# Attention and gated feed-forward on one core: batches 0 and 1 by head halves and tile pairs, w_out loaded in one go, a new order table

## The chip, the cores and the metric

The kernel runs on one core of one Trainium2 chip. The metric is the device time of one execution in microseconds; the median of 3 runs of the kernel before is 281.9 us (281.62 to 282.12).

## What is computed

For each of 8 batches and 8 heads, a linear attention with position weights: q and k go through a ReLU and are multiplied by cos and sin of the position, so that 64 features become 128; kv is the sum over the sequence of k' times v, z the sum of k'; each output row is q' kv / (q' z + 1e-6). The heads side by side are a token's 512 values x, for 8 x 576 = 4608 tokens. Then a feed-forward layer with a gate:

```python
q_p = phi(q, cos_w, sin_w)
k_p = phi(k, cos_w, sin_w)
kv = np.einsum('bhsf,bhsd->bhfd', k_p, v)
z = np.sum(k_p, axis=2)
num = np.einsum('bhsf,bhfd->bhsd', q_p, kv)
den = np.einsum('bhsf,bhf->bhs', q_p, z)[..., None] + 1e-06
x = (num / den)          # to (4608, 512)
h = x @ w_in             # (512, 2048)
out = (h * np.cos(h)) @ w_out   # (2048, 512)
```

## The kernel before

The feed-forward layer runs over nine chunks of 512 tokens: four tiles of 128 from each of the eight batches, and a ninth chunk of what is left of all of them. `layer1(c)` multiplies chunk c by w_in and applies the gate (ACT computes cos as a shifted Sin, L502; DVE or GpSimd multiplies, L504); `layer2(c)` multiplies by w_out. From chunk 3 on parts of layer 1, and from chunk 1 on all of layer 2, save products in Strassen's manner with sums made ahead (`w_out_sums`, L809; L861 and L667 are those matmuls). Layer 1 of chunks 0 and 1 (L529) works in 16 groups of eight matmuls of 256 columns: per quarter of w_in, per half of the tokens, two column pairs. The three banks M1 of PSUM are used in turn. Layer 2 of chunk 0 is plain (`layer2_plain`, L786): eight groups of eight matmuls of 512 columns, four token tiles for the first half of w_out and four for the second; ACT copies the first (L794), DVE adds the second (L797).

A batch's attention: SyncE (SP) loads q, k and v (`load`, two DMAs each, L318 and L321; v of batches 0 and 1 in head halves, four DMAs). `prep` (L346 on ACT, L347 on DVE) makes q' and k' in f16, one instruction per tile and factor with all 8 heads (128x512); `cast_v` (L360 to L362) makes v in f16. PE transposes q' (L402), forms kv (L373) and the numerators with z in a 65th column (L435); DVE normalises (L451 adds 1e-6, L453 inverts, L455 multiplies); PE transposes x (L475) and ACT copies it to xT (L479). From batch 2 on the DMA transposes q' and, later, x.

The beginning: `first_attention` (batch 0) loads q, k and v and has PE run fill matmuls on a constant tile (`warm`, L945) where it would be idle. `weights` holds w_in's four quarters, loaded by GpSimd (POOL) with a cast (L956), until batch 0's keys have landed: a small copy (L950) writes into w_in_sb and reads the keys, so that the DMA waits for it. In the same way a copy (L960) lets w_out's first two quarters go (L970) when w_in's first quarter has landed. `second_attention` (batch 1) holds its loads by small copies on POOL that read w_in's third quarter (`hold_raw`, L975; `GATE1`), and w_out's last two quarters by one that reads batch 1's queries (`part_of_w_out`, L982).

The order of all work is written out by hand. Every step is recorded by `pl.add` with an engine or a choice of them, what it reads and what it writes; `Plan.run` sorts the 1363 steps by the table STARTS and takes each one's engine from the table ENGS. Each engine then runs its steps in that order, one after the other, and waits by semaphores for what a step reads. PE, ACT, DVE, POOL and SP have one queue each; the DMAs that SP issues run in the profile's queue 1, those of POOL in queue 0.

## Time and profile before

| what | value |
|---|---|
| median of 3 runs | 281.9 us (281.62 to 282.12) |
| the profiled execution, from its first to its last instruction (its span; its own time is listed as no more than this) | 279.7 us |
| median above that span | 2.2 us |
| PE busy | 272.6 us (97%) |
| DVE / ACT / POOL busy | 236.9 / 210.2 / 82.9 us |
| granted TensorE clock | 1.000 |
| batch 0's first layer-1 matmul | 21.20 us |
| PE without interruption on layer 1 of batch 0 from | 23.88 us |
| batch 1's first layer-1 matmul | 50.27 us |
| chain: last PE work to the end of the span | 273.27 to 279.7 us |
| w_in issued by POOL | 11.13 to 14.58 us |
| w_out issued by POOL | 17.75 to 19.23 us and 38.49 to 40.15 us |
| batch 1's loads issued by SP | 25.88 to 33.81 us |

The page gives busy time per engine, the chain of work that ended last (followed back from the last instruction, at each step to what released it), groups of instructions by source line, and the DMA issues with their time to landing. Answers about a part of the trace give the same for a stretch: the timeline merges instructions of one line on one engine, and gives in brackets the idle time of the engine before them and what ended it; "SPq" and "POOLq" are DMA issues. In `x8` at a line's end, 8 is a count.

### The profile page before, as it was taken

What the parts mean: (1) busy time and instruction counts of PE and PEld (TensorE: products, weight loads), DVE (VectorE), ACT (ScalarE), POOL (GpSimd) and SP (SyncE); (2) the same over time, 40 slices, a digit from 0 to 9 for tenths busy, and PEclk for the clock granted to TensorE, in tenths of its full rate; (3) what the DMA queues carried; (4) which work ended last, traced back from release to release, by engine and by line L of the source; (5) the groups of instructions that cost most, each with busy time, mean ns of one, the idle gap of its engine ahead of it and who ended that gap; (6) DMA issues with size and microseconds to landing.
All of it is one profiled execution on the core that took longest, in us unless ns stands there. A gap on an engine that the chain in (4) does not pass through costs nothing.

```text
span 279.7 us, 6825 instructions
## 1 busy us (share of the span) xinstructions
PE 272.6 (97%) x2698; PEld 215.5 (77%) x2698; DVE 236.9 (85%) x442; ACT 210.2 (75%) x363; POOL 82.9 (30%) x102
## 2 busy tenths in 40 slices
PE   8999999999999999999999999999999999999993
PEld 2567857787966677769777878789988888888882
DVE  1767698989999999999999998989989879873952
ACT  2756699879998897788989988995758686776330
POOL 1430020030501201520340045132534372399210
PEclk9999999999999999999999999999999999999999
DMA  6999989999999999989999998549756495698125
GB/s 207 312 202 206 340 239 241 361 301 174 335 261 271 258 249 246 234 268 259 255 258 246 242 229 284 98 115 141 163 75 139 110 156 105 152 143 123 75 77 150
DMA packets 80223, 58.03 MB, mean 207 GB/s; under 512 B 43200, under 2 KB 77248, under 8 KB 80192
## 3 DMA queue, kind: packets, MB, share of 16 engines
q1 hardware_dynamic: 68960, 39.99, 59.4%
q0 software_dynamic: 10496, 17.04, 30.1%
q10 hardware_dynamic: 736, 0.57, 0.7%
q8 instruction: 21, 0.34, 0.5%
q14 instruction: 10, 0.08, 0.1%
HBM read 36.75 MB, written 11.80 MB: 174 GB/s over the span
## 4 chain that ended last, share of the span: by engine, by line
PE 92%; ACT 3%; DVE 2%; issue 1%; POOL 0%; ACTq 0%; POOLq 0%
PE M L861 34%; PE M L667 14%; PE M L561 11%; PE M L529 9%; PE TR L667 6%; PE ATT L945 5%; PE ATT L435 3%; PE M L786 3%; PE ATT L373 3%; PE TR L561 2%; ACT KQ L346 2%; DVE x L455 1%; PE M L402 1%; PE M L373 0%; PE TR L475 0%
## 5 line engine op out<-in xcount | busy, mean ns | idle before, releaser
L861 PEld LDWEIGHTS <-gT 128*128 128x128 f16 x560 | 53.9, 98 | 8.3
L861 PE MATMUL M<-w_out_sb,gT 128*128 128x256 f16 x448 | 57.1, 273 | 0.0
L504 DVE TENSOR_TENSOR gT<-M,ch 128x512 f16<-128x512 f32 x73 | 48.5, 685 | 5.9 <-ACT ch L502 5.7
L502 ACT ACTIVATE ch<-M 128x512 f32<-128x512 f32 x75 | 43.4, 596 | 12.0 <-PE M L529 5.4
L346 ACT ACTIVATE KQ<-km,CS 128x512 f16<-128x512 f32 x57 | 38.5, 717 | 1.4 <-DMA km<-in_k_dram 1.3
L872 ACT ACTIVATE ost<-M 128x512 f32<-128x512 f32 x41 | 24.3, 596 | 17.9 <-PE M L861 13.0
L346 ACT ACTIVATE KQ<-qm,CS 128x512 f16<-128x512 f32 x46 | 31.5, 720 | 4.1 <-DMA qm<-in_q_dram 4.1
L561 PE MATMUL M<-xT,w_in_sb 128*128 128x512 f16 x136 | 33.8, 379 | 0.0
L861 PE MATMUL M<-T,S 128*128 128x256 f16 x256 | 32.4, 273 | 0.0
L667 PEld LDWEIGHTS <-w_in_sb 128*128 128x128 f16 x288 | 27.3, 98 | 4.8 <-issue 0.3
L362 POOL CAST V<-vm 128x1024 f16<-128x1024 f32 (+1 forms) x18 | 15.9, 907 | 50.8 <-DVE den L451 20.7
L529 PE MATMUL M<-xT,w_in_sb 128*128 128x256 f16 x256 | 30.3, 273 | 0.3 <-DVE gT L504 0.3
L861 PEld LDWEIGHTS <-S 128*128 128x128 f16 x256 | 24.8, 98 | 4.1 <-DVE S L837 0.2
L529 PEld LDWEIGHTS <-w_in_sb 128*128 128x128 f16 x256 | 24.4, 98 | 3.9 <-issue 0.5
L679 DVE TENSOR_TENSOR Z<-M,Z 128x512 f32<-128x512 f32 x31 | 21.1, 687 | 4.3 <-PE M L667 3.1
L561 PEld LDWEIGHTS <-w_in_sb 128*128 128x128 f16 x160 | 14.9, 98 | 12.2
L504 POOL TENSOR_TENSOR gT<-Z,ch 128x512 f16<-128x512 f32 x5 | 6.3, 1268 | 56.6 <-ACT ch L502 20.0
L455 DVE TENSOR_TENSOR x<-ATT,rec 128x512 f16<-128x512 f32 x32 | 22.1, 691 | 1.1
L435 PEld LDWEIGHTS <-qT 128*128 128x128 f16 (+1 forms) x320 | 14.8, 101 | 5.6 <-issue 3.5
L690 ACT ACTIVATE ch<-Z 128x1024 f32<-128x1024 f32 x12 | 12.7, 1057 | 6.9 <-DVE Z L679 4.8
L675 ACT ACTIVATE Z<-M 128x512 f32<-128x512 f32 x26 | 15.1, 596 | 3.4 <-PE M L667 2.4
L435 PE MATMUL ATT<-kvz,qT 128*128 128x65 f16 (+1 forms) x288 | 16.0, 195 | 0.8 <-DVE x L455 0.5
(150 smaller groups left out, 519.3 us busy)
## 6 DMA issues: line engine op xcount, KB each, us to landing
out_dram<-ost POOLq DMA_DIRECT2D x38, 256.0 KB, 4.3
qm<-in_q_dram SPq DMA_DIRECT2D x8, 640.0 KB, 6.7
km<-in_k_dram SPq DMA_DIRECT2D x8, 640.0 KB, 7.1
qm<-in_q_dram SPq DMA_DIRECT2D x8, 512.0 KB, 6.0
km<-in_k_dram SPq DMA_DIRECT2D x8, 512.0 KB, 6.0
vm<-in_v_dram SPq DMA_DIRECT2D x6, 640.0 KB, 5.7
vm<-in_v_dram SPq DMA_DIRECT2D x6, 512.0 KB, 4.6
w_in_sb<-in_moe_w_in_dram POOLq DMA_DIRECT2D x4, 512.0 KB, 8.8
```

The costliest lines, as they stand in the source:

```text
L346: fn = {"ACT": lambda: nc.scalar.activation(out=out_, in_=in_, func=AF.Relu, scale=sc), "DVE": lambda: nc.vector.tensor_scalar(out=out_, i ...
L362: "POOL": lambda: nc.gpsimd.tensor_copy(out=out_, in_=in_)}
L435: nc.tensor.matmul(bank[hb][ps, hh * D1:(hh + 1) * D1], lhsT=x[:, h, :], rhs=z[:, h, :], start=True, stop=True)
L455: nc.vector.tensor_tensor(out=split(x16[n][:, hs, :], k), in0=A[:, :, :, 0:D], in1=split(rec[n][:, hs], k).unsqueeze(3).broadcast_to((P, k ...
L502: act(0.5, due, lambda: nc.scalar.activation(out=ch[c], in_=bank, func=AF.Sin, bias=math.pi / 2.0, scale=1.0), [key], [("ch", c)])
L504: mul(due, 0.61, lambda q: q.tensor_tensor(out=dst, in0=bank if len(dst.shape) == 2 else bank.rearrange("p (j s) -> p j s", j=dst.shape[1] ...
L529: nc.tensor.matmul(M1[m][:, jj * 2 * P:(jj + 1) * 2 * P], lhsT=w_in_sb[:, cc, j * P:(j + 1) * P], rhs=X[:, cc, ts], start=(cc == 0), stop= ...
L561: nc.tensor.matmul(M, lhsT=w_in_sb[:, cc, j * P:(j + 1) * P], rhs=X[:, cc, :], start=(cc == 0), stop=(cc == NCT - 1))
L667: nc.tensor.matmul(bank[0][:, j * TH:(j + 1) * TH], lhsT=a(cc, j), rhs=b[:, cc, :], start=(first and j == 0 and cc == 0), stop=(last and j ...
L679: dve(0.61, due + 0.3, lambda: nc.vector.tensor_tensor(out=dst, in0=bank[0], in1=dst, op=ALU.add), [bank[1], key], [key])
L861: nc.tensor.matmul(bank[0][:, tt * MH:(tt + 1) * MH], lhsT=a[:, j, tt * P:(tt + 1) * P], rhs=b[:, j, :], start=(first and (apart or tt == ...
L872: act(0.5, due, lambda: nc.scalar.activation(out=dst, in_=view(bank), func=AF.Copy), [bank[1]], dk)
```

## The change

Batch 0 is worked on in `first_attention_halves`. q is prepared as before; k, v, kv, the numerators and x go by head halves (4 heads): all of the first half, then all of the second. k's preparations and V's casts are of 128x256 (a cast of two tiles 128x512), on the engine that the table names. The numerators of two tiles share the two banks ATT, and one normalisation serves both tiles of a half (128x512); x goes to xT by two tiles and one half of the channels. The loads are the same DMAs; what releases w_in is the same (the keys). Fill matmuls: 20 recorded at the start, 12 behind the first half's kv, two behind each pair of numerators (the table puts some of them elsewhere): 40 in all for 54.

Layer 1 of chunks 0 and 1 runs two quarters of w_in for the first half of the tokens, then for the second, then the other two quarters.

Batch 1 has kv by halves in ATT, numerators and x by pairs and halves, V's casts by halves on DVE, ACT or POOL.

`HOLDW` is -1: all four quarters of w_out are issued behind w_in when w_in's first quarter has landed. `RAW1` is 6: batch 1's loads are released by the landing of w_out's third quarter. den, rec and x16 become slices of one tile each. STARTS and ENGS are new throughout, for 1375 steps. Options of `OPT` that are 0 or empty (F16, MODE, DA, SQ) leave the code as it was.

```diff
+OPT = dict(F16=0, FAST1={3: 2, 4: 2, 5: 2, 6: 4, 7: 4, 8: 4}, MODE={}, HH='kv', LD=[['q', 3], ['k', 3], ['v',
+           0], ['v', 1]], NB=[['A0', 'A1'], ['A0', 'A1', 'M0']], XB=[['B3'], ['B3', 'M1']], W0=5, W1=6,
+           WF=[[2, 2], [2, 2]], HOLD=['k', 0], P0=1, RAW1=6, WO2=-1, H1=2, DA=0, W2=0, SQ=0, NUZ=1)
...
-    GATE1 = (w_in_sb[0:2, 0, Dff // 2 + 1:Dff // 2 + 2], [("w_in", 2)])
+    R1 = OPT["RAW1"]
+    GATE1 = ((w_in_sb[0:2, 0, R1 * Dff // 4 + 1:R1 * Dff // 4 + 2], [("w_in", R1)]) if R1 < 4 else
+             (w_out_sb[0:2, (R1 - 4) * NJT // 4, 1:2], [("w_out", R1 - 4)]))
+    HOLDW = OPT["WO2"]
...
-            for quarter in range(4):
-                for hf in range(2):
+            for quarter, hf in ([(q_ + i, hf) for q_ in (0, 2) for hf in range(2) for i in range(2)] if OPT["HH"] else
+                                [(q_, hf) for q_ in range(4) for hf in range(2)]):
+                if True:
...
-            w_out_load(0, 2)
+            w_out_load(0, 2 if HOLDW >= 0 else 4)
...
+    def kv_half(hb, bank, key, due, b=0):
+        hs = range(H)[HALVES[hb]]
+        full[key] = False
+
+        def mm():
+            for hh, h in enumerate(hs):
+                for t in range(NT + 1):
+                    nc.tensor.matmul(
+                        bank[:, hh * D1:(hh + 1) * D1], lhsT=kp[:, t, h].rearrange("p g d -> p (g d)"),
+                        rhs=V1[:, t, h, :], start=(t == 0), stop=(t == NT))
...
+        copy_by_either(Z[:, hb], bank[:, 0:HB * D1], due, 0.4, 0.38, [key], [("kvz", b, hb)])
...
+    def num_pair(i, hb, due, b=0):
+        hs = HALVES[hb]
+        for t in (2 * i, 2 * i + 1):
+            bank, key = ATT[:, t % 2, :], ("ATT", t % 2)
...
+        def norm():
+            nc.vector.tensor_scalar_add(out=denp[:, n], in0=A[:, :, :, D], scalar1=1e-6)
+            nc.vector.reciprocal(out=recp[:, n], in_=denp[:, n])
+            nc.vector.tensor_tensor(out=XF[:, hb, 2 * i:2 * i + 2], in0=A[:, :, :, 0:D],
+                                    in1=recp[:, n].unsqueeze(3).broadcast_to((P, 2, HB, D)), op=ALU.mult)
+        dve(1.05, due, norm, [("ATT", 0), ("ATT", 1)], [("XF", b, i, hb)] + ([("XF", 0, i, hb)] if b else []))
+
+    def x_pair(i, hb, bank, key, due, b=0):
...
+        def mm():
+            for j in range(2):
+                x2 = XF[:, hb, 2 * i + j].rearrange("p h d -> p (h d)")
+                for c in range(NCT // 2):
+                    nc.tensor.matmul(ps[:, c, j * P:(j + 1) * P], lhsT=x2[:, c * P:(c + 1) * P], rhs=IDENT,
+                                     is_transpose=True)
...
+    def half_tiles(hb, due):
...
+            if nm == "k":
+                for t in range(NT + 1):
+                    for g in range(2):
+                        prep(0, "k", t, g, "", due, hs)
+            elif nm == "v":
+                for t, nt in ((0, 2), (2, 2), (4, 1)):
+                    cast_v(0, t, ("DVE", "ACT", "POOL"), due, hs, nt=nt)
+                kv_half(hb, *BANKS2[hb], due)
...
+        if hb == 0:
+            for i in range(OPT["W1"]):
+                warm(2, 0.4314, ATT[:, 1, :], [("TR", 0)] if i == 0 else [], [("ATT", 1)])
+        if OPT["P0"]:
+            for i in range(NT // 2):
+                num_pair(i, hb, due + 2 * i)
+                n = OPT["WF"][hb][i]
+                if n:
+                    warm(n, 0.2157 * n, M1[1], [("ATT", 1)], [("M1", 1)])
+                x_pair(i, hb, *pick[kb_[i % len(kb_)]], due + 2 * i)
+            return
...
+    def first_attention_halves():
...
+        for i in range(OPT["W0"]):
+            warm(4, 1.293)
+        for nm, x in OPT["LD"]:
+            load(0, nm, 0, HALVES if x == 2 else (slice(0, H),) if x == 3 else (HALVES[x],))
+        weights()
...
+        for hb in range(2):
+            half_tiles(hb, 4 + 4 * hb)
...
     def second_attention():
...
-            if nm == ORDER1[HOLDW]:
+            if HOLDW >= 0 and nm == ORDER1[HOLDW]:
                 part_of_w_out(nm, 1)
...
+            if OPT["HH"]:
+                for t, nt in ((0, 2), (2, 2), (4, 1)):
+                    cast_v(1, t, ("DVE", "ACT", "POOL"), T + 4 + hb, HALVES[hb], nt=nt)
+                continue
...
+        if OPT["H1"]:
+            for hb in range(2):
+                kv_half(hb, ATT[:, hb, :], ("ATT", hb), T + 6, 1)
+            if OPT["H1"] == 2:
+                for i in range(NT // 2):
+                    for hb in range(2):
+                        num_pair(i, hb, T + 8 + 2 * i, 1)
+                        x_pair(i, hb, *(BANKS[3], BANKS[2])[hb], T + 8 + 2 * i, 1)
...
-    first_attention()
+    (first_attention_halves if OPT["HH"] else first_attention)()
```

More of the change, by code (lines that the diff above doesn't have):

```diff
@@ L362, in cast_v @@
               "POOL": lambda: nc.gpsimd.tensor_copy(out=out_, in_=in_)}
-        either(due, {e: cost[e] for e in ([eng] if eng else VCAST)}, fn, rd, wr)
+        either(due, {e: cost[e] for e in ([eng] if isinstance(eng, str) else eng)}, fn, rd, wr)
+    full = {}
     def kv(b, due, pair=None):
@@ L378, in kv @@
             hs = range(hb * HB, (hb + 1) * HB)
+            full[keys[hb]] = False
             pe(HB * (NT + 1), MMA, due, lambda hb=hb: mm(hb),
@@ L398, in q_pe @@
         ps = bank.bitcast(F16).rearrange("p (h s) -> p h s", h=H)
+        more = [("qTh", t % NT, hb) for hb in range(2)] if b <= 1 and OPT["HH"] else []
         def mm():
@@ L438, in num @@
         for hb in range(2):
+            full[keys[hb]] = False
             pe(HB * len(parts), MMA, due, lambda hb=hb: mm(hb), rd, [keys[hb]])
@@ L577 @@
     LATE = min(c for c, nf in FAST1.items() if nf > 2)
-    assert all(FAST1[c] == NJT // 4 for c in range(LATE, NC))
     def flat(t, dt=F16):
@@ L946, in warm @@
         pl.add("PE", us, us, -1, go, rd, wr)
+        pl.steps[-1]["ni"] = n
     def weights():
```

288 lines of the change are left out of this document (231 added, 57 removed), and 197 rows, old and new, of the table STARTS.

## The prediction

> **What bounds the kernel now.** I read the page first: TensorE (PE) is busy for 272.6 of 279.7 us and the chain of waits is PE for 92% of the span. A busy PE is not one at its peak, so I looked next at the chain in order of time, at the stage that the change touches (columns: start us, duration us, what):
>
> ```profile
> PE 92%; ACT 3%; DVE 2%; issue 1%; POOL 0%; ACTq 0%; POOLq 0%
> ```
>
> ```profile
> 22.48 0.76 DVE x L455 x2
> 23.23 0.61 DVE gT L504
> ...
> 23.88 10.72 PE M L529 x96
> ...
> 34.67 0.45 issue
> 35.12 1.60 ACT KQ L346 x3
> ...
> 43.70 0.57 ACT kvz L390
> ...
> 50.43 1.64 PE M L529 x15
> ```
>
> The reader is to see two places where something other than PE sets the pace. Up to 23.88 it is batch 0's attention (DVE's normalisation, L451 to L455). From 35.12 to 44.27 it is ACT on batch 1's attention, and that stretch begins when batch 1's keys land. From 50.27, where the first multiplication of batch 1's layer 1 stands in the timeline, PE is never idle for 24.73 us (busy 24.73 of 24.73 in the view by stretches). So the question is when PE comes to that point, and how much work it then has left.
>
> When the keys land is read from the timeline, the one-microsecond stretches (after the colon: length, busy us of PE, PEld, DVE, ACT, POOL, granted clock, DMA share, GB/s), and the DMA issues (KB each, us to landing):
>
> ```profile
> 17.75 1.48 POOL L970 DMA_DIRECT2D w_out_sb<-in_moe_w_out_dram  x2 [0.30 <-POOL w_out_sb L960]
> 25.67 0.18 POOL L975 CAST km<-w_in_sb 2x1 f32<-2x1 f16 x1 [6.44 <-ACT ch L502]
> 25.88 0.60 SPq L321 DMA_DIRECT2D km<-in_k_dram  x1
> ```
>
> ```profile
> 28.00:29.00 1.00, 1.00 (x12) 0.90 (x10) 0.78 (x2) 0.72 (x2) 0.00 (x0) 1.00 1.23 207
> 29.00:30.00 1.00, 1.00 (x12) 0.90 (x10) 0.69 (x1) 0.71 (x2) 0.00 (x0) 1.00 1.12 319
> ```
>
> ```profile
> vm<-in_v_dram SPq DMA_DIRECT2D x1, 320.0 KB, 8.0
> ```
>
> The keys' load was issued at 25.88, but the engines moved at the weights' rate (205 GB/s) until 29; between 25.8 and 27.2 the DMA view lists queue 0 (POOL's) alone. Batch 1's loads waited for the whole w_out half queued before them. The keys' second part, issued at 26.59, took 8.0 us and landed at 34.6; the last part of v, issued at 32.95 with the 8.0 of the line above, at 40.9.
>
> **Step 1, batch 0's attention.** The loads and the release of w_in (keys at 10.5) stay. 54 fill matmuls become 40; they stood where PE waited, so they are worth nothing. k is prepared and v cast in head halves: an instruction of 128x256 starts every 0.20 us on DVE and 0.31 on ACT (V casts in the timeline), one of 128x512 every 0.40 and 0.62, so halves cost no more in sum. From 10.53: DVE's seven half preparations 1.4, two delays of 0.13 beside POOL's DMA issues (a preparation took 0.61 there against 0.48), V casts 0.6 with a wait for v at 12.1: first half's kv at 12.9 to 13.7, kvz at 14.1, four fill matmuls to 14.5, numerators 0.25. Then four normalisations, each of two tiles and one half, at 1.11 each (L451 at 18.84 to the end of L455 at 19.95), with the numerators (0.35) between: 14.75, 16.25, 17.8; the third ends at 18.9. Transposes and copy to xT take 0.9, and layer 1 starts at 19.9 against 21.2. Bounds: 19.3 without the fill in between, 21.2 if a half costs as much as a whole. Before, PE still lost time among the first groups: the third starts at 23.88, which with 0.87 a group is a stream from 22.1. After, one transpose (0.23) is left in it: a stream from 20.1. **-2.0 us at this point.**
>
> **Step 2, layer 1 of batch 0 by token halves.** The built kernel's order puts the 15th group into the bank of the 13th, with one group between. A group's bank is free 2.4 us after its start (25.69 to 28.09: matmuls, Sin, multiplication), two groups take 1.75: **+0.7**, not seen before. Layer 2 begins at 33.9. Its first four weight quarters: in POOL's built order they go first, third, second, fourth, so the "third quarter" is the second in the queue. It lands when the second one landed before, at 18.48 + 12.3 = 30.8; the other two, at 512 KB by 205 GB/s = 2.56 each, at 33.3 and 35.9. PE wants the second quarter at 34.8: 1.5 of cover. DVE's T3, which wants all four, stands behind the last multiplication and ahead of k's preparation; both wait anyway.
>
> **Step 3, batch 1's loads.** Released at 30.8, issued at 31.2, and behind two w_out quarters as before: everything moves by two quarters, 5.1 to 5.4 (2.56 by rate, 2.7 by the distance of the landings). Keys at 39.8, queries at 43.1, last v at 46.1 to 46.3 against 40.9. The waiting instructions are SP's loads and POOL's four small copies; behind them in their queues stand only batch 2's loads and V casts, which need batch 1's anyway. Gone is w_out's second half at 38.5 to 48.7, so batch 2's loads follow at once.
>
> **Step 4, what PE does meanwhile.** Before, five of layer 2's eight groups (1.73 each, L786) came ahead of batch 1's layer 1, three behind it. After, all eight come ahead, six before the attention and two between its parts. From 33.9: six groups and the last layer-1 group give 45.2. Then, in the built order: query transposes at 45.2 and 46.05 (ACT's four query preparations of 0.62 from 43.4), first kv at 46.5, second at 47.3 when POOL has cast its part of v's second half. That cast is of 128x256 and 128x512; the latter took 0.62 (row at 66.34), the former lies between 0.2 and 0.62: 1.0 together, 0.8 to 1.2. kv 0.62 and latency, kvz 0.4 on ACT: numerators 48.6, normalisation 1.11, transposes and numerators 50.4, layer 2 1.73, 0.5, layer 2 1.73, numerators and transposes 0.5: batch 1's layer 1 at **54.85**. PE idles 1.6 us in it, all of it behind the late v. Ends: 54.2 if every cast and copy follows the data at once, 55.6 if v lands at 46.5 and an addition to ost (0.69) goes ahead of kvz on DVE.
>
> **Step 5, the sum.** Before, PE is at this point at 50.27, with three groups of layer 2 (5.2) more to do, less a transpose (0.23) that is still to come after: equal work at 55.2. 54.85 - 55.2 = **-0.4 us**. So the 2.0 of step 1 are spent: 0.7 on the bank, the rest waiting for v. Two terms nearly cancel: data 5.2 later, 5.2 of layer 2 in front. Behind it the instructions are the same in kind and number. ACT is the tight one: 22.63 of 24.73 busy from 50.27 on. With layer 2's three groups gone the stage is 5.2 shorter, but the built order has eight of batch 2's preparations (0.62 each, 5.0) on ACT ahead of batch 1's first Sin: nothing either way.
>
> 279.7 - 0.4 = 279.3 for the profiled span; the median of the runs, 281.9, is 2.2 above that span, and what lies around it is untouched: **281.5 us**. By the ends of steps 3 and 4: 280.8 to 282.3.
>
> **Rivals.**
> *The start's gain comes through.* Against it: the chain at 35.12 begins at a landing, and loads waited for queue 0 a second time (batch 2's keys, issued at 42.20, while the DMA view for 43 to 46 lists queue 0 and not theirs). For it: DMA work is only bounded by two cases. If v is there when PE is (needs it by 44.5), 45.2 + 4.6 of attention + 3.5 of layer 2 = 53.2: -2.0, 279.9. Half of it is likelier than all: 280.5.
>
> *ACT is late in batch 1's layer 1 (slower).* Place: the 16 groups back to back from 54.85, each with a Sin of 0.60 in 0.87 of PE. If batch 2's keys, which now follow v at some 49.4, come too late for the eight preparations to be done before the first Sin, PE waits for ACT: up to 22.6 - 19.5 = 3.1, half of it 1.5: 283.0. It decides from three preparations left over (1.9 us). For it: ACT is busy 92% and DVE as much in that stage. Against: the keys' own preparations there can go to either engine.
>
> *PE's slow phase lasts longer.* In this run PE's first 14 matmuls took 0.43 us a piece, up to 7.18, then 0.216, though the granted clock reads 1.00. After, only 16 fill matmuls precede the transposes (8.0 to 10.2) and there are gaps. If the step to full speed comes after the fill, transposes and ten more fills cost 2 us more; the wait for v hides 1.2 of it: +0.8 on the forecast, 282.3. The Trainium skill (TensorE: Matmul & The Clock Gate, Part 1) says that full speed comes after a busy window of about 3.4 us, that the window runs free, and that the number of slow matmuls therefore differs from run to run; the trace has one such start only, 5.9 us long.
>
> *The release does nothing.* Since loads wait for queue 0 to drain, opening them at the second or the third quarter gives the same landing: that is in the forecast, not beside it.
>
> **Chances.** Forecast 0.48 (of it faster 0.15, same 0.29, slower 0.04), start's gain 0.25 (faster), ACT late 0.21 (slower), slow phase 0.06 (same 0.02, slower 0.04). What a measurement of this kernel can tell from no change is 0.2%, 0.56 us. Faster 0.40, same 0.31, slower 0.29. The range reaches to the gain's half and to ACT's 1.5: 280.2 to 283.2.
>
> **What would show it.** Step 1: first multiplication of layer 1 at 19.3 to 20.6. Step 2: PE idle about 0.7 us near 32.5. Step 3: w_out's issues back to back, keys prepared from 39.8, queue 1 silent until 34. Step 4: PE idle 1 to 2 us between 45 and 50, batch 1's layer 1 at 54.2 to 55.6. Step 5: PE without gaps from there. Keys prepared before 38.5 make it wrong towards faster; PE gaps before Sin results between 55 and 72 towards slower.

## Result, and the profile after

The changed kernel takes 285.2 us (median of 4 runs, 284.54 to 285.50) against 282.0 (281.62 to 282.47): a ratio of 1.0108, 95% interval 1.0091 to 1.0126. It is slower, by 3.2 us. The prediction said 281.5, with a range of 280.2 to 283.2. The profiled execution's span is 283.3 us against 279.7, its own time 285.21.

PE's share of the chain of waits falls from 92% to 86%; DMA, which was not in that row, has 5%: the load of batch 0's keys at the start, which the chain before did not go through, and a transpose of q', 7.7 and 7.6 us:

```profile
PE 86%; DMA 5%; DVE 4%; ACT 1%; issue 1%; SPq 1%; DVEq 0%
```

The chain in order of time (start, duration, what), where it leaves PE (pieces called "issue", of 0.02 to 0.04 us each, are left out between the lines):

```profile
15.99 0.08 DVE den L1189
...
19.18 0.18 DVE den L1189
...
47.82 1.22 PE ATT L1130 x40
49.07 0.44 DVE kvz L1108
49.55 0.30 PE ATT L1182 x4
49.88 0.40 ACT kvz L1109
50.31 0.30 PE ATT L1182 x4
...
62.78 7.64 DMA qT<-KQ
70.47 0.30 PE ATT L457 x4
```

The reader is to see three things. Batch 0's first normalisation starts at 15.9 (15.99 in the chain, 15.91 in DVE's timeline; the prediction had 14.75), its third at 19.18 (17.8). From 49.07 to 50.31 the chain goes DVE, PE, ACT, PE in single file: the second copy of kv out of PSUM (kvz, ACT) starts only after the first four numerators, though neither needs the other. And from 69 on PE waits for the DMA transpose of q' of batch 2's second tile, issued at 62.78 and landed 7.64 us later.

The loads came as forecast. POOL's small copies are released at 30.98 (they read the w_out quarter that landed at 30.86; the bracket names DVE, whose multiplication came last by the profile), SP issues the first load behind them, and the engines go from the weights' rate to a higher one at 34 to 35 (before: 29; columns as in the prediction, all engines):

```profile
30.98 0.18 POOL L1063 CAST km<-w_out_sb 2x1 f32<-2x1 f16 x1 [10.38 <-DVE gT L542]
```

```profile
31.19 0.60 SPq L336 DMA_DIRECT2D km<-in_k_dram  x1
```

```profile
33.00:34.00 1.00, 1.00 (x9) 0.78 (x8) 0.30 (x1) 0.60 (x1) 0.00 (x0) 1.00 1.26 210
34.00:35.00 1.00, 0.61 (x7) 0.49 (x6) 1.00 (x3) 0.60 (x1) 0.00 (x0) 1.00 1.14 288
35.00:36.00 1.00, 1.00 (x9) 0.61 (x7) 1.00 (x2) 0.44 (x1) 0.00 (x0) 1.00 1.10 373
```

Keys landed at 39.33, queries at 42.60, the last v at 45.73. The 0.39 us that PE is not busy in the second row is the wait for the 15th group's bank.

Where the 3.6 us of span come from, by the start times of PE's matmuls (idle time is the distance between two starts less the usual distance):

| point | predicted | measured | difference, cumulated |
|---|---|---|---|
| batch 0's third layer-1 group | 21.85 (stream from 20.1) | 23.26 | +1.41 |
| 14th and 15th group's bank | 0.7 | 0.7 | +1.41 |
| layer 2 begins | 33.9 | 35.31 | +1.41 |
| PE at batch 1's query transposes | 45.2 | 46.55 | +1.35 |
| PE idle from there to batch 1's layer 1 | 1.6 | 2.1 | |
| batch 1's layer 1 | 54.85 | 56.80 | +1.95 |
| idle near 58 and 59 | 0 | 0.7 | +2.7 |
| wait for the DMA transpose at 70.47 | 0 | 1.4 | +4.1 |

-0.4 predicted and +4.1 make +3.7; the span says +3.6.

### The profile page after: what moved, and what is told of

It is laid out like the page before. It is cut to its first block, busy times and chain, and to the rows that moved or that the text cites. A ratio compares the mean times of both kernels' runs of the same rounds, so it can differ in the third digit from the quotient of the medians.

```text
span 283.3 us, 6808 instructions
## 1 busy us (share of the span) xinstructions
PE 271.1 (96%) x2684; PEld 214.1 (76%) x2684; DVE 236.9 (84%) x433; ACT 211.6 (75%) x365; POOL 83.1 (29%) x103
## 4 chain that ended last, share of the span: by engine, by line
PE 86%; DMA 5%; DVE 4%; ACT 1%; issue 1%; SPq 1%; DVEq 0%
PE M L945 34%; PE M L729 14%; PE M L601 10%; PE M L568 7%; PE TR L729 6%; PE M L870 5%; DMA km<-in_k_dram 3%; DMA qT<-KQ 3%; PE ATT L457 3%; PE ATT L390 2%; PE TR L601 2%; DVE KQ L362 1%; DVE XN L1191 1%; PE ATT L1182 1%; SPq L336 0%
## 5 line engine op out<-in xcount | busy, mean ns | idle before, releaser
L361 ACT ACTIVATE KQ<-km,CS 128x512 f16<-128x512 f32 (+1 forms) x63 | 41.3, 686 | 0.6 <-DMA km<-in_k_dram 0.6
L361 ACT ACTIVATE KQ<-qm,CS 128x512 f16<-128x512 f32 x45 | 30.6, 722 | 4.3 <-DMA qm<-in_q_dram 4.3
L377 POOL CAST V<-vm 128x1024 f16<-128x1024 f32 (+2 forms) x20 | 16.7, 867 | 55.0 <-DVE KQ L362 23.0
L478 DVE TENSOR_TENSOR XN<-ATT,rec 128x512 f16<-128x512 f32 x28 | 19.4, 691 | 1.0
L827 POOL DMA_DIRECT2D out_dram<-ost x12 | 13.3, 1200 | 11.1 <-ACT ost L956 11.1
L362 DVE TENSOR_SCALAR KQ<-qm,CS 128x512 f16<-128x512 f32 x27 | 12.0, 481 | 5.5 <-DMA qm<-in_q_dram 5.4
```

What stands on the lines that cost most here:

```text
L361: fn = {"ACT": lambda: nc.scalar.activation(out=out_, in_=in_, func=AF.Relu, scale=sc), "DVE": lambda: nc.vector.tensor_scalar(out=out_, i ...
L377: "POOL": lambda: nc.gpsimd.tensor_copy(out=out_, in_=in_)}
L478: nc.vector.tensor_tensor(out=split(x16[n][:, hs, :], k), in0=A[:, :, :, 0:D], in1=split(rec[n][:, hs], k).unsqueeze(3).broadcast_to((P, k ...
```

## Experiments

All are edits of the changed kernel unless said otherwise, so all times compare with 285.2 us and, in the same session each, with the kernel before; the ratio is to the latter. In STARTS, step numbers count the recorded steps, values are hundredths of a planned microsecond; only the order matters. "Lands" and "starts" are of the profiled execution, which is one of the runs; between the profiled executions the moment at which batch 0's keys land differs by up to 0.7 us (10.31 to 10.97; e8: 12.08) and shifts everything up to batch 1 with it.

### The start

**e3: weights released later.** `HOLD=['k', 0]` becomes `HOLD=['v', 0]`.

> Only change: w_in's four loads are released by the first landed part of v (about 12.3) instead of the keys (10.6), so POOL issues them at about 13.0 to 16.1. Theory (POOL's DMA issues hold up DVE): no instruction of DVE between 10.6 and 12.9 takes longer than 0.40, where four half preparations and casts took 0.51, 0.62, 0.76 and 0.69 before; the long ones move behind 13. kv's first half then starts about 0.6 earlier than its second matmul group at 13.99. Rival (the v loads or the casts themselves slow DVE): the same instructions stay long at the same place. Either way the weights and batch 1's loads behind them come 1.5 to 1.8 later; the whole is expected at 285 to 287 us. Half preparations stay at 0.26 apart on DVE and 0.40 on ACT in both.

284.8 us (one run). DVE's timeline, changed kernel:

```profile
10.67 2.38 DVE L362 TENSOR_SCALAR KQ<-km,CS 128x256 f16<-128x256 f32 x7
12.97 0.96 DVE L376 CAST V<-vm 128x256 f16<-128x256 f32 x2
13.85 0.94 DVE L362 TENSOR_SCALAR KQ<-km,CS 128x256 f16<-128x256 f32 x2
```

and e3's, with POOL's issues:

```profile
10.66 1.93 DVE L362 TENSOR_SCALAR KQ<-km,CS 128x256 f16<-128x256 f32 x7
12.51 0.62 DVE L376 CAST V<-vm 128x256 f16<-128x256 f32 x2
13.04 0.61 DVE L362 TENSOR_SCALAR KQ<-km,CS 128x256 f16<-128x256 f32 x2
```

```profile
13.49 3.16 POOL L1044 DMA_DIRECT2D w_in_sb<-in_moe_w_in_dram  x4 [0.31 <-POOL w_in_sb L1037]
```

The same eleven instructions take from 10.66 to 13.65 instead of 10.67 to 14.79: with POOL's issues (3.16 us, from 11.26 in the changed kernel) moved away, they are 1.1 us faster. In the changed kernel three half preparations beside those issues take 0.51, 0.62 and 0.69 us instead of 0.34, and a V cast 0.76 instead of 0.42; half preparations at 15.32 and 16.94, when the weights are on their way but POOL issues nothing, take 0.34, so the moving weights are not the cause; and in e3 the one at 16.08, now beside the issues, takes 0.69. Layer 1 starts at 20.63 instead of 21.29. The theory holds. The weights, and batch 1's loads behind them, are some 2 us later (v lands at 48.01), PE waits 1.3 for w_out at 45.6, and the gain is spent; no transpose is waited for here. With one run, 284.8 can't be told from 285.2.

**e7 and e8: another order of the start.** Four half preparations and casts of the second half go behind normalisations, four fill matmuls are left out; in e7 on top of e6 below, in e8 alone.

```diff
-W0=5, W1=6
+W0=5, W1=4
+STARTS[82], STARTS[74], STARTS[85] = 1441, 1442, 1443   # 1141, 1369, 1393
+STARTS[76], STARTS[32] = 1544, 1215                     # 1543, 1300
```

> As e6_dve_order, and batch 0 in another order: on DVE four preparations and casts of the second head half go behind the first half's normalisations, the copy of qT ahead of others, and four fill matmuls between the first half's kv and its numerators are left out. Theory (the start is set by DVE's order of half preparations, beside POOL's DMA issues): first normalisation at 14.9 to 15.3 instead of 15.9, layer 1 of batch 0 at 20.5 to 20.9 instead of 21.3; of the 0.4 to 0.8 gained little comes through at batch 1, where v (landed 45.8) and its casts on ACT (done at 48) hold kv: the time 0 to 0.4 below e6. Rival (the start's gain comes through, as in the prediction's first rival): 0.5 to 0.8 below e6.

> The changed kernel with the other order of batch 0 alone (as in e7_start; batch 1's banks and the stores as in the changed kernel). Theory: layer 1 of batch 0 at 20.5 to 20.9; kv of batch 1 then waits for ACT's V casts, so that 0 to 0.4 of it are left at batch 1's layer 1, and the wait for the transpose near 69 takes up the rest: 284.7 to 285.4 us. Rival: the gain comes through, 284.3 to 284.7.

284.32 (1.0072, 1.0051 to 1.0093) and 285.31 us (1.0091, 1.0064 to 1.0117). In e7 the first normalisation does come earlier, 4.5 us behind the keys' landing (15.25 and 10.76) instead of 5.3 (15.91 and 10.57), but the third is at 19.25, and layer 1 at 21.36: 10.60 behind the keys instead of 10.72. The second half waits for the work that the first has passed. A miss: 0.1 gained, not 0.4 to 0.8. e8's profiled execution, the longest of its eight (286.60), had its keys at 12.08, and the granted clock was 0.50 from 17.8 to 21.2 (see the last section); it says nothing of what the order is worth.

**e17: keys prepared in whole tiles.**

```diff
-                for t in range(NT + 1):
+                for t in range(0 if hb else NT + 1):
                     for g in range(2):
-                        prep(0, "k", t, g, "", due, hs)
+                        prep(0, "k", t, g, "", due)
+DROP = steps 74 to 83 (the second half's ten preparations)
```

> The changed kernel with batch 0's keys prepared in whole tiles (10 instructions of 128x512 where each half had 10 of 128x256), all of them ahead of the first half's kv; everything else by halves as in the changed kernel. Theory (a half costs 0.26 on DVE and 0.40 on ACT, two thirds of a whole at 0.40 and 0.61, so halving buys the first half's start with work that the second half has to wait for): first normalisation 0.2 to 0.6 later than 15.9, but the second half's kv no longer waits for preparations; layer 1 of batch 0 at 21.0 to 21.5 against 21.3, the time 285.0 to 285.5 us, no difference to 285.2. Rival (the prediction's step 1: the halves bring the start forward): layer 1 at 21.8 to 22.5, and the time 0.5 or more above 285.2.

285.43 us (1.0106, 1.0076 to 1.0135), the same as with halves. First normalisation on DVE, and PE:

```profile
15.90 0.17 DVE L1193 TENSOR_SCALAR den<-ATT 128x8 f32<-128x8 f32 x1 [0.98 <-PE ATT L1186]
```

```profile
14.59 1.03 PE L1035 MATMUL ATT<-S 128*128 128x512 f16 x4
15.45 0.42 PE L1186 MATMUL ATT<-kvz,qT 128*128 128x65 f16 x8
...
21.30 0.93 PE L572 MATMUL M<-xT,w_in_sb 128*128 128x256 f16 x7
```

Layer 1 starts at 21.30 against 21.29: halving the keys' preparation is worth nothing here. With whole tiles DVE has 0.98 us to spare ahead of the first normalisation, and the numerators stand behind four fill matmuls (14.59 to 15.45). In the changed kernel DVE was busy through to 15.9. So, as the two timelines read, two different limits give the same time.

### The ties at batch 1

**e2: kv of batch 1 in two banks of their own.**

```diff
-                kv_half(hb, ATT[:, hb, :], ("ATT", hb), T + 6, 1)
+                kv_half(hb, *BANKS[2 + hb], T + 6, 1)
```

> Only change: batch 1's kv halves go into the banks M1_2 and TR instead of the two banks of the one tile ATT. Theory (the tile ties the banks): the copy of the first half's kv (kvz, DVE) then starts at 48.4 instead of 49.07, right behind its own half; that of the second half (ACT) at 49.0 instead of 49.88; numerators at 48.9 instead of 49.55, and the first normalisation, behind two other instructions of DVE (0.39 and 0.60), at 49.8 instead of 50.71. Batch 1's layer 1 starts 0.7 to 1.0 earlier, at 55.8 to 56.1, and the time falls by 0.5 to 1.0 from 285.2 us. Rival (late data or a late ACT): the copies wait for the V casts and for ACT's queue; kvz moves by less than 0.3, the normalisation by less than 0.3, the time by less than 0.3.

285.51 us (1.0126, 1.0098 to 1.0154; single runs 284.37 to 287.29). DVE, ACT and PE near 49:

```profile
48.59 0.43 DVE L1108 CAST kvz<-M 128x260 f16<-128x260 f32 x1
```

```profile
49.20 0.39 ACT L1109 ACTIVATE kvz<-TR 128x260 f16<-128x260 f32 x1 [0.18 <-PE TR L1130]
```

```profile
49.08 0.41 PE L1182 MATMUL ATT<-kvz,qT 128*128 128x65 f16 x8
```

Each copy now follows its own half, and the eight numerators go in one piece at 49.08 instead of in two at 49.55 and 50.31. ATT is one tile with two banks; with kv and numerators in it, readers and writers of different banks had waited for one another. (One wait was a true one: the numerators of the second tile go into the bank that the second copy reads. e2 takes that away too and does not tell the two apart.) Layer 1 of batch 1 starts at 56.01 instead of 56.80, as the theory has it. The total did not follow: PE, now earlier, waits longer for the same transpose (it goes on at 70.41, the changed kernel at 70.47). In the profiled execution (286.73) PE then also runs at half speed; of the six runs it alone has a mean clock of 0.991 (the others 0.997 or more), so this is not what the median shows. PE's timeline, and stretches of PE (length, busy us and matmuls of PE, granted clock, DMA share, GB/s; the other engines' columns are left out):

```profile
70.41 0.30 PE L457 MATMUL ATT<-kvz,qT 128*128 128x65 f16 x4 [1.95 <-DMA qT<-KQ]
```

```profile
68.00:70.00 2.00, 0.46 (x5) 1.00 1.42 103
70.00:72.00 2.00, 1.59 (x20) 0.85 0.99 308
72.00:74.00 2.00, 2.00 (x11) 0.50 1.11 341
74.00:76.00 2.00, 2.00 (x23) 0.80 1.16 340
```

After that wait the granted clock is 0.50 from 71.4 to 74.8: the 16 layer-1 matmuls from 72.11 on take 3.07 us to the next one's start, where the same 16 take 1.75 in the changed kernel (71.83 to 73.58). By matmul starts this cost another 1.7 us.

### Stores and transposes

**e1: three stores of batch 0 later.** `STARTS[239], STARTS[244], STARTS[245] = 7181, 7182, 7183` (5868, 5923, 5978).

> Only change: three of batch 0's four output stores (L814), which POOL issued at 61.94 to 63.00, are issued behind POOL's V casts of batch 3, at about 76 us. Theory (stores beside the transposes): the DMA transpose of q' that PE waited for took 7.64 us because the stores held the engines between 64 and 68; without them it takes 4.2 to 6 as the others do, lands by 69, and the 1.40 us of PE at 69.07 to 70.47 go: 283.8 to 284.2 us against 285.2. Rival (issue time): the transposes are late because the first of them is issued only at 61.40, when PE has done the numerators of batch 1's last tile (54.3 in the kernel before), and batch 3's keys are still being moved then; the second still lands after 69.8 and the time stays within 0.4 of 285.2.

285.68 us (1.0130, 1.0113 to 1.0146). SP's issues, and PE:

```profile
61.53 4.90 SPq L440 DMA_TRANSPOSE qT<-KQ  x3
```

```profile
69.21 0.29 PE L463 MATMUL ATT<-kvz,qT 128*128 128x65 f16 x4
...
88.45 0.30 PE L463 MATMUL ATT<-kvz,qT 128*128 128x65 f16 x4 [0.54 <-DMA qT<-KQ]
...
94.98 0.30 PE L463 MATMUL ATT<-kvz,qT 128*128 128x65 f16 x4 [0.27 <-DMA qT<-KQ]
```

The first transpose is issued no earlier (61.53 against 61.40), yet the second lands at 66.05 instead of 70.43, and the wait at 70.47 is gone. So the stores made it late, not the issue. But at 76 the stores lie ahead of batch 3's transposes; by matmul starts PE waits for transposes for 0.7 us at 88, 0.4 at 95 and 0.7 at 111, and for a normalisation for 0.4 at 92. The mechanism was right and the total wrong.

**e5: e2's banks, one store earlier, two where the kernel before had them.** `STARTS[239], STARTS[244], STARTS[245] = 4779, 7001, 7002`.

> The changed kernel with batch 1's kv in the banks M1_2 and TR (as in e2_untie) and three stores of batch 0 moved: the second one to right behind the first (about 51 us), the other two to behind the first V cast of batch 3 (about 74 us, where the kernel before had them). Theory (two waits, each with a cause of its own, and stores that must not lie beside the transposes): batch 1's layer 1 starts at 56.0 (0.8 earlier), DMA transposes land at 65 and 66, PE does not wait near 69, no loss near 88: 282.6 to 283.4 us against 285.2. Rival (the DMA engines are full from 57 to 90, so whatever is moved collides): one of the numerators of batch 2 or 3 waits for its transpose again, 0.5 us or more, and the time stays at 284 us or more.

284.21 us (1.0056, 1.0027 to 1.0085): 1.0 less than the changed kernel. The second transpose of batch 2 takes 3.21 us (e2, with the same banks and the stores at 61.3: 8.36). The waits of the tie and of that transpose are gone (0.9 stays ahead of the first normalisation), a new one of 1.0 is at 93.9, for batch 3's transposes. The rival's condition held.

**e6: DVE's order at batch 1.** On top of e5, `STARTS[235], STARTS[188] = 4950, 4494` (4704, 4665), and the two stores behind step 235.

> As e5_untie_stores, and on DVE the preparation of batch 1's last q tile goes ahead of a copy of qT (into idle time at 46.4), an addition to ost behind batch 1's second normalisation. Theory (after the tie DVE's own order is late): the first normalisation starts at 49.1 to 49.3 instead of 49.8, batch 1's layer 1 at 55.3 to 55.6, the time 0.3 to 0.6 below e5. Rival (numerators wait for the copy of qT on ACT, or layer 2 waits for the addition that frees its bank): less than 0.2 below e5, PE idle ahead of a group of layer 2 near 51.

284.22 us (1.0065, 1.0043 to 1.0086). A miss: by the profile the preparation that was moved waited 1.12 us for a V cast of POOL, and held up the copy of qT and kvz behind it on DVE. Layer 1 of batch 1 came 0.4 later than in e5.

### Banks and PE's order

**e10 and e14: the 15th group's bank.** In both, the 15th and the 16th group change places, with Sin and multiplication (steps 143 to 145 and 146 to 148). e14 also exchanges the multiplications of the 12th and 13th group (`STARTS[136], STARTS[139] = 3166, 3227`; 3227, 3166), and has e5's edits.

> The changed kernel with the 15th and the 16th group of batch 0's layer 1 changed over (with their Sin and multiplication), so that the banks are used in turn throughout. Theory: the 0.55 of PE's idle time at 34.44 is gone, layer 2 begins 0.55 earlier, and since PE and not the data is late at 46.55, some 0.5 reaches batch 1's layer 1; the wait for the DMA transpose near 69 gives part of it back: 284.6 to 285.2 us. Rival (batch 1 is held by ACT's V casts): all of it is lost again ahead of kv near 47 to 48, 285.2.

> As e5_untie_stores, and batch 0's 15th layer-1 group in the bank that is free, with the multiplications of the 12th and 13th group in that order (as in e11, where PE had no idle time there and layer 2 began 0.5 earlier). Theory (PE, not the data, is late at batch 1): 0.5 to 0.8 earlier at batch 1's layer 1 than e5, and 0 to 0.6 of it at the end, since batch 2's V casts hold its kv (done at 62.0, PE there at 63.0) and the wait near 94 stays: 283.6 to 284.2 us. Rival: batch 1 is held by its own v, nothing at layer 1 of batch 1, 284.2.

e10: 285.45 us (1.0138, 1.0107 to 1.0168); PE waits 1.15 there instead of 0.55, since DVE multiplied the 13th group ahead of the 12th, whose bank was now wanted. e14: 283.05 us (1.0037, 1.0017 to 1.0057), the best of all, with no wait there, layer 1 of batch 1 at 55.23 and 0.5 us left of the wait near 92:

```profile
30.80 4.03 PE L582 MATMUL M<-xT,w_in_sb 128*128 128x256 f16 x34
34.66 1.67 PE L884 MATMUL M<-w_out_sb,gT 128*128 128x512 f16 x7
...
92.27 0.30 PE L471 MATMUL ATT<-kvz,qT 128*128 128x65 f16 x4 [0.36 <-DMA qT<-KQ]
```

**e9, e11, e12, e16: PE's order at batch 1.** In short, on top of e5 and e10 (e9) or of e14 (e11, e12, e16):

```diff
-                        x_pair(i, hb, *(BANKS[3], BANKS[2])[hb], T + 8 + 2 * i, 1)
+                        x_pair(i, hb, *(BANKS[2] if (i, hb) == (0, 1) else BANKS[3]), T + 8 + 2 * i, 1)   # e9: [hb ^ i]
-            q_pe(1, NT, *BANKS[3], "ACT", start[1] + 10)
+            q_pe(1, NT, *BANKS[0], "ACT", start[1] + 10)
+STARTS[242], STARTS[240] = 4825, 4931   # e9, e11, e12: layer 2 ahead of transposes of x (4931, 5151)
+STARTS[219], STARTS[220], STARTS[222], STARTS[221] = 5345, 5372, 5600, 5601   # e16: the last q tile alone
```

Further, in e9, e11 and e12 the transposes of the last q tile and the first layer-1 group go ahead of the last numerators of pairs; in e9 the third layer-1 group goes ahead of the second. ACT's and DVE's steps for all these are in the same order. In e12 STARTS[244] and STARTS[245] are as in the changed kernel.

> As e5_untie_stores, and further: batch 0's 15th layer-1 group in the bank that has been free longest (it changes places with the 16th); one group of layer 2 ahead of batch 1's first transposes of x and the other ahead of the second numerators, where PE waited 0.9 for the normalisation; the transposes of the last q tile and its numerators ahead of the second layer-1 group, in another bank, so that the DMA transposes of batch 2 are free 2 us earlier; the third layer-1 group ahead of the second, whose bank was waited for (0.40). Theory (what is lost are waits that the order makes, not the late v): no idle near 34.5 (0.55), 51 (0.9), 57 to 59 (0.7); the same work is done at 58 instead of 59.5, batch 2's DMA transposes are issued from 59 instead of 61, and the wait at 93.9 (1.0 in e5) is gone or halved: 281.6 to 282.8 us. Rival (v and its casts, done at 48, hold batch 1, and the DMA engines hold what follows): PE waits longer between 45 and 48 and near 90, and the time stays within 0.5 of e5's 284.2.

> As e5_untie_stores, with both 15th-group and batch-1 orders mended over e9 and e10. In e10 the 15th group was given the 12th group's bank, but DVE multiplies the 13th group ahead of the 12th, so it waited 1.15 instead of 0.55; here those two multiplications change places as well. In e9 the third layer-1 group went ahead of the second, so that a later group took a bank with one group between and PE stood for 2.71; here the second stays second, x of the second tile pair goes through TR, and DVE and ACT gate the groups in PE's order. Theory: no idle time over 0.2 near 34, layer 2 begins at 34.7, no idle near 51 and near 57 to 59, tail numerators done by 58 and batch 2's DMA transposes issued from 59; 1.5 to 2.2 less than e5 at 60: 282.2 to 283.0 us, and if the wait near 94 goes with it 281.5. Rival (the DMA engines hold what follows): what is gained by 60 is waited for at batch 2's or batch 3's numerators, 283.5 to 284.5.

> As e11_order, but two of batch 0's stores stay where the changed kernel had them, right behind POOL's V casts of batch 2 (about 61 us) instead of 74; only the second store is earlier. Theory (stores cost where transposes are under way): the first two transposes are issued at 58.7 to 60.5 and land before or beside the stores by 65; PE's margin for the second is 68, so there is no wait near 68 and less DMA work between 74 and 79, so that the wait near 94 is below 0.5: the same as e11 or up to 0.7 faster. Rival: the second or third transpose is held up by the stores to 68.5 or later, 0.5 to 1.5 slower than e11.

> As e14_bank15_mended, and the transposes of batch 1's last q tile ahead of the last transposes of x, in the bank M1_0, the two transposes of x of the second tile pair both through TR, the last tile's numerators ahead of the third layer-1 group, and ACT's and DVE's steps for these in the same order. Theory: the idle 0.29 and 0.40 of PE near 56 and 57 (a normalisation, and a copy of x that still holds the bank) are gone, and the DMA transposes of batch 2, held until the last tile's numerators are done, are issued at 58.3 to 58.8 instead of 59.83, so that batch 3's are earlier too and the 0.52 near 92 shrinks: 282.0 to 282.6 us, within 0.2% of the kernel before. Rival (batch 2's and 3's data are late by the loads, as e11 and e13 had it): what is gained by 60 is lost between 62 and 95, 283 us or more.

e9: 288.46 us (1.0224, 1.0200 to 1.0248). Its third layer-1 group was put ahead of the second, so that a later group took a bank with one group between, and PE stood 2.7 us at 63.8; the granted clock was 0.50 behind it (63.7 to 67.1). e11: 286.08 (1.0121, 1.0079 to 1.0164; single runs 283.48 to 287.39); e12: 284.35 (1.0074, 1.0049 to 1.0099). Both start batch 1's layer 1 at 54.5 and, after 1.1 us of waiting for a copy of x on ACT, are still 1.7 ahead of the changed kernel for the same work (the fourth layer-1 group) at 59; at 64 only 0.3 is left, after 0.6 for a bank and 0.85 for batch 2's V casts, which POOL had done at 63.5. With two stores at 63.5 and 64.0 (e12) the second transpose is issued at 61.15 and lands at 70.45, and PE waits 1.7 there; with these stores at 74 (e11) it lands at 66.45, but PE waits 0.6 and 1.75 for transposes at 93.7 and 110.7, and e11's median is the higher by 1.7, which neither expectation had. e12's wait is this one:

```profile
70.50 0.30 PE L486 MATMUL ATT<-kvz,qT 128*128 128x65 f16 x4 [1.53 <-DMA qT<-KQ]
```

e16: 283.86 us (1.0055, 1.0036 to 1.0074; single runs 282.52 to 286.16): the idle times near 56 and 57 are gone, 0.6 comes back at 60, and in the profiled execution, the longest of its runs, transposes are waited for at 94 (1.3) and 111 (1.9).

**e13: SP's order.** On e14, `STARTS[331], STARTS[431], STARTS[432] = 6260, 6265, 6268` (6532, 6717, 6833): batch 2's fourth transpose and batch 3's queries ahead of batch 3's v.

> As e14_bank15_mended, and in SP's queue the fourth DMA transpose of batch 2 and the loads of batch 3's queries go ahead of the loads of batch 3's v. Theory (the wait near 94 comes from SP's order: batch 3's queries are issued behind the transposes, so their preparation and transposes are late): the queries of batch 3 land at 73.5 to 75 instead of 75.2 to 77.0, the first transpose of batch 3 is issued near 79 instead of 80.5, no wait over 0.3 near 94: 0.7 to 1.0 below e14, 282.5 to 283.2 us. Rival (the data of batches 2 and 3 as a whole are late since batch 1's loads start later; moving one forward moves another back): v of batch 3 is late instead, or transposes still land late, a wait of 0.5 or more stays between 80 and 110: 283.5 to 284.3.

286.86 us (1.0176, 1.0153 to 1.0198). The queries land at 72.1 and 74.0, as meant, v at 77.2 instead of 72.0, and kv waits for its casts:

```profile
80.47 0.22 PE L407 MATMUL ATT<-V,KQ 128*128 128x65 f16 x2 [1.81 <-POOL V L394]
```

```profile
82.00:84.00 2.00, 2.00 (x14) 0.55 0.95 279
```

The clock is halved again behind that wait. POOL issues two stores, 1.05 us from 78.30 on, between the V casts of this wait, since they stand behind the first of them; so by the timeline part of the wait is theirs and not the late v's. The rival had the mechanism; its time (283.5 to 284.3) was too low.

### The loads

**e4: batch 1's loads released as before.** `RAW1=6` becomes `RAW1=2`.

> Only change: batch 1's loads are released by w_in's third quarter (landed 23.0) as in the kernel before, while all of w_out stays ahead of them in the weights' queue; SP issues them from about 23.5 instead of 31.2. Theory (nothing of SP's queue moves until the weights' queue has drained): queue 1 moves nothing before about 33.5, keys land at 37.3 to 39.5 as with the release at w_out's third quarter (37.53 and 39.33), the time stays within 0.4 of 285.2 us. Rival (the queues share the engines): keys land by 33, w_out's last quarters later than 38, and layer 2's second half waits for them: up to 2 us slower.

286.56 us (1.0158, 1.0142 to 1.0174). SP issues from 23.24. Queues from 27 to 31, then PE's first wait for w_out:

```profile
q0 software_dynamic: 506, 0.50, 75.2%
q1 hardware_dynamic: 440, 0.45, 40.3%
```

```profile
37.23 2.10 PE L870 MATMUL M<-w_out_sb,gT 128*128 128x512 f16 x9 [1.15 <-DMA w_out_sb<-in_moe_w_out_dram]
```

Queue 1 did not wait for the weights to be done: from 27.3 on, 4 us behind the issue, the two queues moved packet for packet (506 and 440). Keys landed at 33.15 and 37.67, w_out's quarters at 28.4, 32.8, 37.2 and 41.6 instead of 28.1, 30.9, 33.4 and 36.4, and layer 2 waited 1.3. The rival was right, and the prediction's reading of the first trace (loads wait until the weights' queue is empty) was wrong: it had seen loads issued only some 3 us ahead of that moment.

**e15: the new loads alone, in the kernel before.**

```diff
-    GATE1 = (w_in_sb[0:2, 0, Dff // 2 + 1:Dff // 2 + 2], [("w_in", 2)])
+    GATE1 = (w_out_sb[0:2, NJT // 4, 1:2], [("w_out", 1)])
-            w_out_load(0, 2)
+            w_out_load(0, 4)
-            if nm == ORDER1[HOLDW]:
-                part_of_w_out(nm, 1)
```

> The kernel before with the new loads alone: all of w_out behind w_in, batch 1's loads released by the landing of the second w_out quarter in the queue (30.8, as in the changed kernel); its own order of everything else. Theory (the loads by themselves cost what they delay, and only an order made for them can hide it): batch 1's keys land at 37.5 to 39.3 instead of 33 to 34.6, its last v at 45.7 instead of 40.9; PE stands still 4 to 5.5 us between 38 and 50, layer 1 of batch 1 starts at 54.3 to 55.8 instead of 50.27, but with three groups of layer 2 still to do, so the time is 286 to 287.5 us. Rival (batch 1's attention was late for ACT's sake, not for the data's, and w_out's second half no longer lies beside batch 1's): less than 2 us slower than before, under 284.

288.20 us (1.0227, 1.0195 to 1.0258): +6.1, more than either expected. DVE, PE and the stretches behind (busy by engine, granted clock):

```profile
39.76 0.49 DVE L352 TENSOR_SCALAR KQ<-km,CS 128x512 f16<-128x512 f32 x1 [5.37 <-DMA km<-in_k_dram]
```

```profile
41.50 1.86 PE L534 MATMUL M<-xT,w_in_sb 128*128 128x256 f16 x8 [4.99 <-DVE gT L509]
```

```profile
36.00:42.00 6.00, 1.01 (x8) 0.67 (x7) 2.24 (x5) 2.16 (x4) 0.00 (x0) 0.78 1.04 356
42.00:44.00 2.00, 2.00 (x9) 1.06 (x8) 1.66 (x6) 2.00 (x5) 0.00 (x0) 0.50 1.09 358
44.00:46.00 2.00, 2.00 (x6) 0.73 (x5) 2.00 (x7) 1.91 (x4) 0.00 (x0) 0.50 0.49 159
46.00:48.00 2.00, 2.00 (x16) 1.14 (x15) 1.55 (x7) 1.89 (x6) 0.00 (x0) 0.94 0.05 16
```

In the old order a preparation of batch 1's keys stands on DVE ahead of two multiplications of batch 0. It waits for the later keys, PE waits for a bank behind them, and the clock is halved from 39.4 to 46.2 (worked out from the rows above: 0.78 on average up to 42, 0.94 from 46 to 48). PE works for 4.7 us at that clock, which costs it some 2.4 on top of the wait of 5.0; this execution, at 289.88, is the longest of four, and the mean clock is 0.984 to 0.992 in all of them. So the load plan in the old order costs 6.1 us, of which the halved clock is a part, and the rest of the change gets back about half of that.

## Why the prediction was wrong, step by step

*Step 1 (batch 0, "-2.0 us at this point")* is mis-sized: the third group starts 0.62 us earlier than before, not 2.0. Three terms failed. A half preparation was priced by the rows of V casts (0.20 and 0.31 apart); it starts every 0.26 on DVE and every 0.40 on ACT in this trace, two thirds of a whole tile's 0.40 and 0.61. The "two delays of 0.13" beside POOL's issues are 1.1 us over the eleven instructions (e3). And the halving of k, the core of the step, gives nothing (e17); by the timelines DVE's work (changed kernel) or the fill matmuls (e17) hold the first normalisation at 15.9 either way.

*Step 2* was right: 0.7 for the bank. e14 shows that it is a matter of order, not of three banks.

*Step 3* was right in its times (keys 39.33 for 39.8, queries 42.60 for 43.1, v 45.73 for 46.1 to 46.3) and wrong in its reason (e4): the times came out by luck, since before and after the loads were issued only some 3 us ahead of the moment at which the weights' queue was done. "The release does nothing" was put aside as certain on that reason; e4 shows that the release decides which load gets the bandwidth.

*Step 4* gave 1.6 us of idle time, "all of it behind the late v". There are 2.1, and none is behind v: PE, late by 1.35 from the start, came to the query transposes at 46.55, behind the last v (45.73). 1.3 are the tie in ATT, 0.6 the first normalisation behind it, 0.2 a preparation of q on ACT. (In e2 the 1.3 go, the wait for the normalisation grows to 0.9, and 0.8 are left as gain.)

*Step 5* failed most: "the instructions are the same in kind and number", "PE without gaps from there". What had moved is when the same DMAs meet. The prediction counted the stores' bytes nowhere: batch 0's stores, at 72.9 to 75 before, are issued at 50.8 and from 61.9 to 63.5: layer 2 is now done earlier, and the new table has three of them right behind POOL's V casts of batch 2, where they meet batch 2's transposes. That costs 1.4 us at this place (gone in e1 and e5, back in e12). 0.7 more near 58 and 59 are a normalisation and a bank still held by a copy of x (gone in e16, which waits 0.6 at 60 instead).

The sum, "data 5.2 later, 5.2 of layer 2 in front": its first half is borne out by the landings (step 3); e15's 6.1 us is not a measure of it, since a part is the halved clock. The rivals: of the start's gain, 0.62 was there and not 2.0; "ACT is late" named the right side, at 283.0 still 2.2 too low, with a mechanism that is not in the trace (no wait of PE for a Sin between 55 and 72); the slow phase did not last (the fill matmuls start every 0.43 us up to 6.74 and every 0.22 from there, ahead of the transposes at 8.16). None named the transposes.

Settled by runs are the price of the loads in the old order, the tie (with the bank that e2 frees as well), the stores beside the transposes, the 15th group's bank, and that halving k gives nothing. PE's idle times over 0.2 us between 21 and 130 add up to 4.7 us in the changed kernel and 2.3 in e14, and of these 2.4 us e14 has 2.1 back. Not settled is the last 1.0 us to the kernel before: the idle times near 50 and 57 that e14 keeps (1.6) went in e11 and partly in e16, but in their one trace each those versions then waited for V casts or for transposes between 60 and 111. Their single runs lie up to 3.9 us apart (e11 283.48 to 287.39, e16 282.52 to 286.16); what differs between them is not shown. No place for the stores was shown to be best, and no version beat the kernel before.

## What to carry to other kernels

When a change moves a stage's end by some microseconds, list every DMA that this stage issues, stores too, and look what it will lie beside; a table of engine work says nothing of that. Price an instruction that is cut in two from a row of the same operation and layout, not of the same size. And when two halves share a tile, their readers and writers may wait for each other even in different banks: a copy released by a matmul that it does not need is the sign in the profile.

## What the runs showed of the hardware

- The granted clock fell to 0.50 in the middle of five profiled executions, each time for 3.4 us (e2 71.4 to 74.8, e8 17.8 to 21.2, e9 63.7 to 67.1, e13 82.2 to 85.6) or twice that (e15 39.4 to 46.2). In the 3.4 us ahead, PE was not busy for 1.95 us (e2), 1.64 (e8, in several waits), 2.46 (e9), 1.99 (e13) and 2.9 (e15). Waits of 1.23 us (changed kernel), 1.59 (e11) and 1.75 (e16; all by the brackets of the timeline) left the clock at 1.00. Why 1.64 in e8 was enough and 1.75 in e16 was not stays open. The 3.4 us at half clock cost PE 1.6 to 1.7 us more in e2 and e13. The Trainium skill (TensorE: Matmul & The Clock Gate, Part 1) puts the return to half clock behind an idle window of about 3.4 us. Here 1.6 to 2.5 us of idle time were enough.
- Two DMA queues share the engines packet by packet (e4: 506 to 440 in 4 us), but a load issued beside the weights moved its first packets only 4 us later (e4), and 3 us later in the changed kernel (31.19 to 34). The Trainium skill (DMA: Bandwidth & Descriptors, Queues, rings and completion order) says that each engine goes round the queues it has work for, a packet at a time. The trace of e4 agrees.
- Four POOL DMA issues of 0.8 to 0.9 us lengthened DVE instructions beside them by 1.1 us in all (e3), all of them preparations and casts from SBUF; normalisations (0.69 us at 17.97 and 19.62), which read PSUM, were not longer beside the issues of w_out (17.64 to 20.61). The Trainium skill (SBUF — State Buffer, Who interferes with whom) names the port pair that DVE and GpSimd share as the only such place, held exclusively. The trace shows who was lengthened and fits with that; it does not show the port.
- Three pairs of kernels differ in the place of the stores alone. The second DMA transpose of batch 2 took 7.64, 8.36 and 9.30 us with stores beside it (changed kernel, e2, e12) and 3.13, 3.21 and 5.35 without (e1, e5, e11). Stores are not all that slows a transpose: the same one took 6.12 in the kernel before and 6.79 in e9, with no store near it.
